# Loading v for two batches per transfer in an attention and spectral-mixing kernel

## The chip, the core and the metric

One core of a Trainium2 chip runs the whole kernel. TensorE (PE in the profile, with its weight loads as PEld), VectorE (DVE), ScalarE (ACT), GpSimd (POOL) and SyncE (SP) each run their own list of instructions in order; POOL and SP also issue the transfers between HBM and the on-chip memory, and 16 DMA engines carry them out. The metric is the device time of one execution in microseconds (us), taken as the median of the runs shown.

## What is computed

The reference, cut to what matters:

```python
scores = scale * q @ k.T                       # q, k, v: (8 batches, 8 heads, 576, 64), float32
cum = cumsum(log(clip(f, 1e-4, 1)))            # f: (8, 8, 576)
scores = where(causal, -1e9, scores + cum[..., :, None] - cum[..., None, :])
x = softmax(scores) @ v                        # then heads side by side: (8, 576, 512)
X = rfft(x, axis=1)[:, :64]                    # 64 modes
Y = X * (w_r + 1j * w_i)                       # per mode a 512 x 512 product, complex
u = x + irfft(Y)
out = u + relu(u @ w_ch)                       # (8, 576, 512), float32
```

The inputs are 9.4 MB each of q, k and v, and 134.2 MB of the mode weights w_r and w_i (64 modes x 512 x 512 x 4 bytes, twice).

## The kernel before

**Stages.** The kernel has two stages. The attention stage is the loop of L552 with 34 iterations over 32 pairs; a pair is one batch b and two neighbouring heads 2g and 2g+1 (L100: g outer, b inner, so pairs 2j and 2j+1 are two neighbouring batches of one g). Iteration i computes the scores and exponentials of pair i, the products with v of pair i-1, and the Fourier sums (`dft`) of pair i-2. The second stage (from L623) takes the mode products with the weights in 16 groups u of 4 modes, each group in four pieces dc, and the last part (from L845) builds the output. Some pieces of the weights are used early, within the attention loop: `spec_early` (L534) takes one from iteration 10 on, two in iterations 10 to 13.

**Transfers.** Nothing schedules the work: instructions stand in the order of the text, engine by engine. Except f and the first v, POOL issues every load; SP issues f, the first v and all stores. In iteration i of the attention loop the loads stand at its head, in this order:

- `load_qk(i + 4)` (L103): q and k of a pair, two transfers, converted to bf16 on the way, into one of 5 buffers. A buffer is free when `trans` (L346) of the pair five before it has read it.
- `issue_half()` (L174): half of a weight piece (512 KB as written, converted from float32), into one of NW = 7 buffers or into a "guest" place that is not used yet (L132).
- `load_v(i + 3)` (L114): v of a pair, float32, 288 KB, into one of 4 buffers. It is free when `scale_v` (L369) of pair i-1 has read it. `scale_v(i + 1)` stands at the end of iteration i.
- a second `issue_half()`, except in iterations 3, 6, 9, 12 and 15.

Before the loop (L229 to L238) SP issues f and v of pairs 0, 1 and 2, while POOL issues q and k of pairs 0 to 3 with three weight halves between them.

**Semaphores.** The framework gives POOL's transfers eight semaphores in turn, so POOL's next transfer waits until the one eight before it has landed; SP's take turns on eight others. In the second stage POOL issues a whole weight piece (two transfers) after each piece used (L814), and waits for the matmuls of `spec_mms` (L180) to free a buffer.

**What reads v.** `scale_v` on DVE multiplies v by a factor per row and writes `vn` in bf16 (L372); `turn_v` (L376) and `back_v` (L388) put `vn` through two transposes on PE into `vs`, the operand of the products of `av` (L469).

```python
        vt = vpool.tile([128, 9, Dh], F32, tag="vt", name="vt")
            v[b, 2 * g : 2 * g + 2, :, :].rearrange("h (c r) d -> (h c) (r d)", r=9),
```

Partition p of the tile holds nine rows r of 64 values: 2304 bytes that lie side by side in HBM, and the 128 partitions follow one another without a gap.

Of the kernel before, what the change touches and what calls it, by code (L numbers as in the profile page):

```python
# [10 lines left out]
F32 = mybir.dt.float32  # L11
BF16 = mybir.dt.bfloat16
I32 = mybir.dt.int32
ALU = mybir.AluOpType
# [3 lines left out]
def _strided(ap: bass.AP, free_dims, offset_elems: int = 0) -> bass.AP:  # L18
    new_ap = [list(ap.ap[0])] + [list(x) for x in free_dims]
    return bass.AP(tensor=ap.tensor, offset=ap.offset + offset_elems, ap=new_ap)  # L20
# [3 lines left out]
def kernel(  # L24
# [12 lines left out]
    B, H, S, Dh = q.shape  # L37
# [8 lines left out]
    NPAIR = B * H // 2  # L46
# [34 lines left out]
    wn = const.tile([128, NPAIR, 9], F32, name="wn")  # L81
# [4 lines left out]
    actx = ExitStack()  # L86
    ssb = actx.enter_context(tc.tile_pool(name="ssb", bufs=1))
    qkpool = actx.enter_context(tc.tile_pool(name="qkpool", bufs=5))
    vpool = actx.enter_context(tc.tile_pool(name="vpool", bufs=4))
    vnpool = actx.enter_context(tc.tile_pool(name="vnpool", bufs=2))  # L90
    vTpool = actx.enter_context(tc.tile_pool(name="vTpool", bufs=1))
    vspool = actx.enter_context(tc.tile_pool(name="vspool", bufs=2))
# [8 lines left out]
    st = [dict() for _ in pairs]  # L101

    def load_qk(i):  # L103
        g, b = pairs[i]
        qk = qkpool.tile([128, 2, S], BF16, tag="qk", name="qk")
        st[i]["qk"] = qk

        for n, src in enumerate((q, k)):
            nc.gpsimd.dma_start(  # L109
                qk[64 * n : 64 * n + 64, :, :],  # L110
                src[b, 2 * g : 2 * g + 2, :, :].rearrange("h (p r) d -> p h (r d)", p=64),
            )

    def load_v(i, eng=None):  # L114

        g, b = pairs[i]
        vt = vpool.tile([128, 9, Dh], F32, tag="vt", name="vt")
        st[i]["vt"] = vt
        (eng or nc.gpsimd).dma_start(
            vt[:].rearrange("p r d -> p (r d)"),  # L120
            v[b, 2 * g : 2 * g + 2, :, :].rearrange("h (c r) d -> (h c) (r d)", r=9),
        )


# [49 lines left out]
    def issue_half():  # L174
        issue_w(whalf[0])
        whalf[0] ^= 1
# [50 lines left out]
    nc.gpsimd.iota(s_i[:], pattern=[[128, NSB]], base=0, channel_multiplier=1)  # L227
    nc.gpsimd.iota(m_i[:], pattern=[[1, 128]], base=0, channel_multiplier=0)
    nc.sync.dma_start(ft, f.rearrange("b h s -> (b h) s"))  # L229
    for i in range(3):  # L230
        load_v(i, nc.sync)
    load_qk(0)
    issue_half()
# [34 lines left out]
    def setup_cum():  # L268
        nc.vector.tensor_tensor_scan(cum[:, 0:S], ones1, lf, 0.0, ALU.mult, ALU.add)
        rref = ssb.tile([BH, 1], F32, name="rref")  # L270
        nc.vector.tensor_copy(rref[:], cum[:, 256:257])
        nc.vector.tensor_scalar(cum[:, 0:S], cum[:, 0:S], rref[:], None, ALU.subtract)
        nc.vector.tensor_copy(cum[:, S : 2 * S], cum[:, 0:S])
        nc.vector.tensor_copy(cum[:, 2 * S : 2 * S + 64], cum[:, 512:576])
# [29 lines left out]
    def setup_small():  # L304
        nc.vector.tensor_scalar(trimask[:], m_f[:], s_f[:, 0:1], None, ALU.is_ge)
        nc.vector.memset(tri4[:], 0.0)
        nc.vector.tensor_copy(tri4[0:64, 0, :], trimask[0:64, 0:64])
        nc.vector.tensor_copy(tri4[64:128, 1, :], trimask[64:128, 64:128])

    def setup_basis():  # L310
        nc.vector.tensor_scalar(bas3[:, :, 0, :], Zt[:, :, :, 1], -1.0, None, ALU.mult)
        nc.vector.tensor_copy(bas3[:, :, 1, :], Zt[:, :, :, 0])
        nc.vector.tensor_copy(bas3[:, :, 2, :], Zt[:, :, :, 1])
# [51 lines left out]
    def widx(i):  # L365
        g, b = pairs[i]
        return 4 * b + g

    def scale_v(i):  # L369
        vn = vnpool.tile([128, 9, Dh], BF16, tag="vn", name="vn")  # L370
        st[i]["vn"] = vn
        nc.vector.tensor_tensor(  # L372
            vn[:], st[i]["vt"][:], _strided(wn[:, widx(i), :], [[1, 9], [0, Dh]]), ALU.mult
        )

    def turn_v(i):  # L376

        tv = psM.tile([128, 9, 64], BF16, tag="m", name="tv")
        for r in range(9):
            for hp in range(2):  # L380
                sl = slice(64 * hp, 64 * hp + 64)
                nc.tensor.transpose(tv[sl, r, :], st[i]["vn"][sl, r, :], ident_bf[sl, sl])  # L382
        st[i]["vT"] = vTpool.tile([128, S], BF16, tag="vT", name="vT")
        nc.vector.tensor_copy(  # L384
            st[i]["vT"][:].rearrange("p (c r) -> p c r", r=9), tv[:].rearrange("p r c -> p c r")
        )
# [25 lines left out]
    def scores(i, T):  # L412

        QT, KT = st[i]["T"][:, 0, :], st[i]["T"][:, 1, :]
        if T == 0:
            st[i]["et"] = epool.tile([128, 3, 2, 512], BF16, tag="et", name="et")
            st[i]["e4"] = epool.tile([128, 64], BF16, tag="e4", name="e4")
            st[i]["m4"] = epool.tile([128, 2, 64], BF16, tag="m4", name="m4")
        if T == 3:
            ps = psM.tile([128, 64], F32, tag="m", name="s4")  # L420
            for hp in range(2):
                sl = slice(64 * hp, 64 * hp + 64)
                nc.tensor.matmul(  # L423
                    ps[sl, :], lhsT=KT[sl, 512:576], rhs=QT[sl, 512:576], start=True, stop=True
                )
            nc.scalar.activation(st[i]["e4"][:], ps[:], ACT.Exp, scale=scale)  # L426
            return
        ps = psS.tile([128, 2, 512], F32, tag="S", name="sps")
        for jb, i0, n, c in SPANS[T]:
            for hp in range(2):  # L430
                sl = slice(64 * hp, 64 * hp + 64)
                nc.tensor.matmul(  # L432
                    ps[:, hp, c : c + n],
                    lhsT=KT[sl, jb * 128 : jb * 128 + 128],
                    rhs=QT[sl, i0 : i0 + n],
                    start=True,
                    stop=True,
                )
        nc.scalar.activation(st[i]["et"][:, T, :, :], ps[:], ACT.Exp, scale=scale)  # L439
# [29 lines left out]
    def av(i, sb):  # L469
        if sb in (0, 3):  # L470
            st[i]["pav"] = psV.tile([128, 3, 2, Dh + 1], F32, tag="av", name="pav")
        pav, vs = st[i]["pav"], st[i]["vs"]
        Ms = SBLK[sb]
        for hp in range(2):
            for jb in range(sb + 1):
                rhs = vs[:, 8, :] if jb == 4 else vs[:, 2 * jb + hp, :]
                nc.tensor.matmul(  # L477
                    pav[:Ms, sb % 3, hp, :],
                    lhsT=eblk(i, hp, jb, sb),
                    rhs=rhs,  # L480
                    start=(jb == 0),
                    stop=(jb == sb),
                )
# [68 lines left out]
    for i in range(NPAIR + 2):  # L552
        live = i < NPAIR
        if i + 4 < NPAIR:
            load_qk(i + 4)
        issue_half()
        if i + 3 < NPAIR:
            load_v(i + 3)
        if i not in less:
            issue_half()  # L560
        prev = i - 1 if 1 <= i <= NPAIR else None
        if live:
            scores(i, 0)
        if i == 0:
            setup_cum()
            setup_small()
        if prev is not None:
            av(prev, 0)
            av(prev, 1)
        if live:  # L570
            scores(i, 1)
        if 0 < i < NPAIR:
            turn_v(i)
        if prev is not None:
            av(prev, 2)
            norm(prev, 0)
        if i + 1 < NPAIR:
            trans(i + 1, 0)
        if live:
            scores(i, 2)  # L580
            if i == 0:
                setup_wn(0, 5)
                setup_wn(5, 9)
                scale_v(0)
                setup_w()
                turn_v(0)
            mask(i, 0)
        if prev is not None:
            av(prev, 3)
        if i + 1 < NPAIR:  # L590
            trans(i + 1, 1)
        if live:
            scores(i, 3)
            back_v(i)
        if prev is not None:
            av(prev, 4)
            norm(prev, 1)
        if live:
            mask(i, 1)
        if i + 1 < NPAIR:  # L600
            scale_v(i + 1)
        if i == 1:
            setup_basis()
        if 10 <= i < 14:
            spec_early(*early[spec_done])
            spec_done += 1
        if i >= 2:
            dft(i - 2)
        if i == 2:
            setup_late()  # L610
        if 3 <= i < 3 + NSB:
            setup_bi(i - 3)
        if i == 3 + NSB:
            setup_bi4(0, 512)
        if i == 4 + NSB:
            setup_bi4(512, 64)
        if i >= 10:
            spec_early(*early[spec_done])
            spec_done += 1
# [3 lines left out]
    with ExitStack() as bctx:  # L623
# [296 lines left out]
        for i in range(len(steps)):  # L920
# [13 lines left out]
            p, sb = steps[i][0]  # L934
# [59 lines left out]
```

## Time and profile before

| | |
|---|---|
| median of 3 runs | 437.77 us (437.42 to 439.06) |
| the profiled execution | 440.27 us |
| its span, first to last instruction | 438.5 us |
| mean granted TensorE clock | 0.938 of full speed |
| busy: PE, DVE, ACT, POOL | 348.4, 268.0, 234.8, 146.1 us |
| moved by the DMA engines | 96.75 MB in 68,414 packets |
| read from HBM, written to HBM | 163.73 MB, 9.44 MB |
| v loads by POOL | 29 of 288 KB, median 10.6 us from issue to landing |
| v loads by SP | 3 of 288 KB, median 7.3 us |

How to read it: a busy time is the sum of an engine's instructions, over stages with different limits. The DMA bytes are counted as written, so a load that turns float32 into bf16 counts half of what it reads; the HBM figure counts what is read. The DMA share adds the times of all packets over 16 engines; two packets of one engine can overlap, so it can exceed 1. In the chain of waits each step goes back to what released it. The attention loop runs from about 10 us to 235 us, the second stage to about 400 us, the output to the end.

### The profile page before, as it was taken

The page shows a single profiled execution, that of the slowest core. Times are in us where ns is not written, and L with a number is a line of the kernel's source. Part 1 is how long each engine was busy: PE and PEld are TensorE (multiplying, and loading weights), DVE is VectorE, ACT ScalarE, POOL GpSimd, SP SyncE. Part 2 cuts the span into 40 slices and gives each one's busy share as a digit, 9 for nine tenths or more (in the row PEclk, how much of TensorE's full clock was granted, in tenths as well). Part 3 has the DMA queues.
Part 4 walks back from the last instruction along what each step waited for, and adds up shares of the span by engine and source line. Part 5 has one row for each costly group of instructions (what it writes and reads, how often), then busy time and mean ns, then how long its engine had stood idle before and what let it go on. Part 6 is the DMA issues. An engine that isn't in the chain of part 4 may idle for free.

```text
span 438.5 us, 10295 instructions
## 1 busy us (share of the span) xinstructions
PE 348.4 (79%) x4264; PEld 191.7 (44%) x4274; DVE 268.0 (61%) x650; ACT 234.8 (54%) x359; POOL 146.1 (33%) x216
## 2 busy tenths in 40 slices
PE   1589877798988988989896484699888598889993
PEld 0355555555555555555563242243333233335330
DVE  4677888867788778888885231222233166455784
ACT  4455776777877756566561022034132166355883
POOL 6454444444544444344214111111122212100283
PEclk9999999999999999999999588599699599699998
DMA  8999999999999999999999999999999999995598
GB/s 180 205 232 221 230 222 232 228 230 228 230 231 224 228 223 227 224 224 223 230 215 212 212 212 212 213 211 212 212 211 212 210 209 210 210 210 106 193 341 331
DMA packets 68414, 96.75 MB, mean 221 GB/s; under 512 B 3600, under 2 KB 45072, under 8 KB 68368
## 3 DMA queue, kind: packets, MB, share of 16 engines
q0 software_dynamic: 62800, 85.64, 105.5%
q1 hardware_dynamic: 5568, 10.47, 6.6%
q8 instruction: 33, 0.54, 0.5%
q14 instruction: 13, 0.11, 0.1%
HBM read 163.73 MB, written 9.44 MB: 395 GB/s over the span
## 4 chain that ended last, share of the span: by engine, by line
PE 40%; DMA 32%; DVE 19%; ACT 3%; issue 3%; POOL 1%; POOLq 0%; ACTq 0%; DVEq 0%
DMA w<-in_moe_w_i_dram 22%; DMA w<-in_moe_w_r_dram 8%; PE pav L477 6%; DVE vT L384 5%; DVE qkT L360 5%; PE A L194 5%; DVE x_all L492 4%; PE pd L521 4%; PE sps L432 4%; PE tv L382 3%; PE vp L393 3%; DMA qk<-in_k_dram 2%; PE U L657 2%; PE s L423 2%; ACT e L426 2%
## 5 line engine op out<-in xcount | busy, mean ns | idle before, releaser
L439 ACT ACTIVATE et<-sps 128x1024 bf16<-128x1024 f32 x96 | 96.0, 1049 | 15.8 <-PE sps L432 12.8
L477 PE MATMUL pav<-vs,et 128*128 128x65 bf16 (+1 forms) x896 | 52.7, 200 | 0.2 <-DVE vn L372 0.2
L360 DVE COPY qkT<-tp 128x640 bf16<-128x640 bf16 x64 | 48.8, 764 | 4.8 <-PE tp L355 4.7
L818 DVE TENSOR_TENSOR Yb<-A,yx 128x512 bf16<-128x512 f32 x15 | 10.4, 691 | 61.6 <-PE A L194 61.6
L477 PEld LDWEIGHTS <-et 128*128 128x128 bf16 (+1 forms) x896 | 37.6, 104 | 18.2 <-issue 13.7
L432 PE MATMUL sps<-qkT 64*128 64x512 bf16 (+4 forms) x320 | 40.3, 315 | 1.1 <-DVE qkT L360 1.1
L697 PE MATMUL pxw<-wch,xT 128*128 128x512 bf16 (+1 forms) x152 | 39.5, 405 | 1.0 <-DVE xT L687 0.4
L194 PE MATMUL A<-w,XP 128*16 128x512 bf16 (+1 forms) x240 | 22.2, 453 | 21.8 <-DMA w<-in_moe_w_i_dram 14.1
L355 PE MATMUL tp<-ident_bf,qk 128*64 128x128 bf16 x576 | 30.6, 238 | 10.9 <-DMA qk<-in_k_dram 10.9
L492 DVE TENSOR_TENSOR x_all<-pav,rcp 128x384 bf16<-128x384 f32 (+2 forms) x96 | 36.2, 377 | 3.3
L384 DVE COPY vT<-tv 128x576 bf16<-128x576 bf16 x32 | 24.2, 757 | 19.7 <-PE tv L382 19.7
L165 POOL DMA_DIRECT2D w<-in_moe_w_r_dram x16 | 11.9, 742 | 70.6 <-PE A L194 50.8
L156 POOL DMA_DIRECT2D w<-in_moe_w_r_dram x27 | 20.4, 757 | 39.9 <-PE A L194 9.1
L704 ACT CAST XW<-pxw 128x512 bf16<-128x512 f32 (+1 forms) x16 | 9.3, 584 | 45.6 <-PE pxw L697 26.6
L404 ACT COPY vs<-vp 128x576 bf16<-128x576 bf16 x32 | 20.5, 639 | 21.9 <-PE vp L400 21.9
L704 ACT CAST yx<-pxw 128x512 bf16<-128x512 f32 (+1 forms) x24 | 14.0, 584 | 32.8 <-PE pxw L697 32.8
L109 POOL DMA_DIRECT2D qk<-in_q_dram x32 | 19.5, 611 | 35.1 <-DMA w<-in_moe_w_r_dram 8.4
L165 POOL DMA_DIRECT2D w<-in_moe_w_i_dram x19 | 13.3, 697 | 52.4 <-PE A L194 23.8
L744 ACT CAST x_all<-pu 128x512 bf16<-128x512 f32 (+1 forms) x40 | 23.4, 584 | 10.6 <-PE pu L743 9.8
L491 DVE RECIPROCAL rcp<-pav 128x6 f32<-128x6 f32 (+2 forms) x96 | 16.2, 169 | 17.7 <-PE pav L477 17.6
L156 POOL DMA_DIRECT2D w<-in_moe_w_i_dram x27 | 20.3, 752 | 18.5 <-DMA w<-in_moe_w_i_dram 8.0
L355 PEld LDWEIGHTS <-qk 128*64 128x64 bf16 x576 | 19.7, 117 | 14.8 <-issue 9.6
(149 smaller groups left out, 685.3 us busy)
## 6 DMA issues: line engine op xcount, KB each, us to landing
w<-in_moe_w_r_dram POOLq DMA_DIRECT2D x16, 1024.0 KB, 29.8
w<-in_moe_w_i_dram POOLq DMA_DIRECT2D x15, 1024.0 KB, 32.4
w<-in_moe_w_r_dram POOLq DMA_DIRECT2D x27, 512.0 KB, 10.9
w<-in_moe_w_i_dram POOLq DMA_DIRECT2D x27, 512.0 KB, 12.4
vt<-in_v_dram POOLq DMA_DIRECT2D x29, 288.0 KB, 10.6
out_dram<-o_sb SPq DMA_DIRECT2D x20, 256.0 KB, 3.2
qk<-in_q_dram POOLq DMA_DIRECT2D x32, 144.0 KB, 10.8
qk<-in_k_dram POOLq DMA_DIRECT2D x32, 144.0 KB, 10.6
```

The costliest lines, as they stand in the source:

```text
L156: nc.gpsimd.dma_start(w8[:, t, :, :], src[4 * u : 4 * u + 4, dc * 128 : (dc + 1) * 128, :].rearrange("m p e -> p m e"),)
L165: nc.gpsimd.dma_start(w8[:, j : j + step, :, :].rearrange("p m r e -> p m (r e)"), src[m : m + step, 256:512, :].rearrange("m (p r) e -> p ...
L194: nc.tensor.matmul(A[32 * j : 32 * j + M, :], lhsT=lhsT, rhs=rhs, start=st_, stop=sp_)
L355: nc.tensor.transpose(tp[64 * hp : 64 * hp + 64, r - r0, :, :].rearrange("p n c -> p (n c)"), qk[:, hp, r * 64 : r * 64 + 64], ident_bf[:, :],
L360: nc.vector.tensor_copy(st[i]["T"][:].rearrange("p n (c r) -> p n c r", r=9)[:, :, :, r0:r1], tp[:, 0 : r1 - r0, :, :].rearrange("p r n c ...
L384: nc.vector.tensor_copy(st[i]["vT"][:].rearrange("p (c r) -> p c r", r=9), tv[:].rearrange("p r c -> p c r"))
L432: nc.tensor.matmul(ps[:, hp, c : c + n], lhsT=KT[sl, jb * 128 : jb * 128 + 128], rhs=QT[sl, i0 : i0 + n], start=True, stop=True,)
L439: nc.scalar.activation(st[i]["et"][:, T, :, :], ps[:], ACT.Exp, scale=scale)
L477: nc.tensor.matmul(pav[:Ms, sb % 3, hp, :], lhsT=eblk(i, hp, jb, sb), rhs=rhs, start=(jb == 0), stop=(jb == sb),)
L492: nc.vector.tensor_tensor(x_all[:ns, g, b, lo:hi, :].rearrange("p s (h d) -> p s h d", h=2), pav[:ns, lo % 3 : lo % 3 + n, :, 0:Dh], _stri ...
L697: nc.tensor.matmul(pxw[rows, :], lhsT=xT[:, eb, sb * 128 : sb * 128 + Ms], rhs=wch[:, eb, :], start=(eb == 0), stop=(eb == NEB - 1),)
L744: nc.scalar.copy(x_all[rows, :, to, sb, :], pu[rows, :].rearrange("p (g c) -> p g c", g=NEB))
```

## The change

`load_v(i)` now loads v of pairs i and i+1 (two batches, the same two heads) in one transfer into a tile with twice the bytes per partition, of which there are two in place of four. SP issues two such loads in the setup, for pairs 0 to 3. In the loop the call stands at the same place, between the two weight halves, in odd iterations 1 to 27 only, for pairs i+3 and i+4. The memory taken is the same (4 x 2304 or 2 x 4608 bytes per partition). Each pair's `scale_v` reads its half of the tile.

```diff
-    vpool = actx.enter_context(tc.tile_pool(name="vpool", bufs=4))
+    vpool = actx.enter_context(tc.tile_pool(name="vpool", bufs=2))
...
         g, b = pairs[i]
-        vt = vpool.tile([128, 9, Dh], F32, tag="vt", name="vt")
-        st[i]["vt"] = vt
+        vt = vpool.tile([128, 2, 9, Dh], F32, tag="vt", name="vt")
+        for k in range(2):
+            st[i + k]["vt"] = vt[:, k, :, :]
         (eng or nc.gpsimd).dma_start(
-            vt[:].rearrange("p r d -> p (r d)"),
-            v[b, 2 * g : 2 * g + 2, :, :].rearrange("h (c r) d -> (h c) (r d)", r=9),
+            vt[:].rearrange("p b r d -> p b (r d)"),
+            v[b : b + 2, 2 * g : 2 * g + 2, :, :].rearrange("b h (c r) d -> (h c) b (r d)", r=9),
         )
...
-    for i in range(3):
+    for i in (0, 2):
         load_v(i, nc.sync)
...
-            vn[:], st[i]["vt"][:], _strided(wn[:, widx(i), :], [[1, 9], [0, Dh]]), ALU.mult
+            vn[:], st[i]["vt"], _strided(wn[:, widx(i), :], [[1, 9], [0, Dh]]), ALU.mult
...
         issue_half()
-        if i + 3 < NPAIR:
+        if i % 2 and i + 4 < NPAIR:
             load_v(i + 3)
         if i not in less:
             issue_half()
```

## The prediction

> **What bounds the kernel now.** I read the chain of waits first, then the DMA rows of the page, then the busy times by stage, then who waits on PE.
>
> The chain that ended last, on the page:
>
> ```profile
> PE 40%; DMA 32%; DVE 19%; ACT 3%; issue 3%; POOL 1%; POOLq 0%; ACTq 0%; DVEq 0%
> ```
>
> Its pieces from 230 us on, the longest of them (start, length, what):
>
> ```profile
> 239.96 34.21 DMA w<-in_moe_w_i_dram
> ...
> 275.58 33.20 DMA w<-in_moe_w_r_dram
> ...
> 310.11 33.56 DMA w<-in_moe_w_i_dram
> ...
> 344.20 29.46 DMA w<-in_moe_w_i_dram
> ...
> 373.70 0.96 PE A L194 x7
> ```
>
> From 240 to 373.7 us the chain is weight transfers alone: each is issued when a buffer comes free and lands some 30 us later. No v transfer stands in the chain. A compute tail follows. Is this a queue that waits for buffers or DMA engines that are full? The busy times by stretch answer (last two columns: DMA share and GB/s as written):
>
> ```profile
> 0.00:5.00 5.00, 0.00 (x0) 0.00 (x0) 3.75 (x10) 1.34 (x2) 4.13 (x12) 1.00 0.55 124
> 5.00:20.00 15.00, 5.90 (x70) 4.25 (x70) 7.33 (x18) 9.03 (x16) 7.24 (x11) 1.00 1.20 213
> 20.00:220.00 200.00, 171.92 (x2909) 112.24 (x2906) 160.81 (x435) 138.80 (x191) 88.61 (x136) 1.00 1.21 227
> 240.00:340.00 100.00, 74.49 (x512) 33.87 (x520) 25.81 (x52) 23.35 (x40) 16.21 (x22) 0.83 1.12 212
> 340.00:390.00 50.00, 40.55 (x229) 16.49 (x229) 23.77 (x38) 24.46 (x43) 8.11 (x13) 0.83 1.17 210
> ```
>
> The engines are full from 5 to 390 us. Counted as read, by the trace's packet records, they read 405 to 410 GB/s in every 20 us of the attention stage and 423 in the weight stage. So the last weight lands when all bytes have been moved, and the end moves only by what the change does to the engine time of the bytes, or by leaving engines empty. PE waits for weights:
>
> ```profile
> PE A L194 <- DMA w<-in_moe_w_i_dram: 14.1, 4, 4.3
> PE tp L355 <- DMA qk<-in_k_dram: 10.9, 2, 9.6
> PE A L194 <- DMA w<-in_moe_w_r_dram: 7.6, 5, 2.7
> ```
>
> The first and third row give 21.7 us: a small shift of the attention stage is taken up there, since weights, not PE, are late behind it.
>
> **The change part by part.**
>
> *POOL's issues.* Removed: 29 v issues of 0.559 us (16.2 us of POOL). Added: 14 of two pairs. Between 0.559 us (128 rows) and 0.757 us (the weight halves' issue, 512 rows) I take 0.62 for 256 rows, 8.7 us. POOL saves 7.5 us, worth nothing: in 20 to 220 us it is busy 88.6 of 200 us and otherwise waits for landings and buffers. SP issues two transfers where it issued three (1.51 us together), hidden too.
>
> *Bytes.* The same. The 28 pairs that POOL still loads are 1792 packets of 4608 bytes now (64 per pair in the records: two rows side by side in HBM). After it, rows of the two batches alternate, so no two neighbours are side by side. The q and k loads, whose rows of 2304 bytes alternate between heads, have one packet per row. I expect the same: 3584 packets of 2304 bytes. Price of a packet cut in two, from the records of stages that are full: 2060 packets of 2048 bytes in a 20 us stretch of the weight stage are 20,000 x 16 / 2060 = 155.3 ns each; a stretch with 1179 of 1024 and 1456 of 2048 bytes then gives (320,000 - 1456 x 155.3) / 1179 = 79.6 ns, so two halves cost 159.2, or 3.9 ns more. 1792 x 3.9 / 16 = **+0.4 us**. Bounds: in the same way the attention stretches give about 90 ns for a q or k row (2304 bytes read) and 203 for a v packet; two rows at 90 save 23 ns: 1792 x 23 / 16 = -2.6 us. Above, SP's rows of 2304 bytes took 123 ns on average against 184 for POOL's packet: +62 ns, over the overlap of 1.21: 1792 x 62 / 16 / 1.21 = +5.7 us. The cut weight packet is nearest, the same bytes in the same full queue.
>
> *Number of transfers.* 32 become 16. Each ends in 16 packets of 4 bytes (3088 and 512 in the records, 20 ns on average), one per engine: 16 x 20 ns = -0.3 us at most; over the overlap, and with 0 as the other end, I take **-0.2 us**.
>
> *Setup.* SP's queue carries 1152 KB in place of 864 while PE waits for the first k (the 10.9 us above, ending at 9.6 and 14.3 us). 288 KB at 285 GB/s, the slowest full microsecond there with SP rows alone, is 1.0 us; the other end is 0, if the queues take turns so that k lands first. The attention stage may start up to 1.0 us later. The 21.7 us hide it; without them it would cost 1.0 us. The bytes come off a later POOL load.
>
> *The new wait.* A v load waited for `scale_v` of pair i-1; now, in odd i, for pair i, one iteration later. Behind it on POOL stand a weight half and the next q and k. Before's issue times against the end of that `scale_v`; the tightest place:
>
> ```profile
> 131.29 0.56 POOL L119 DMA_DIRECT2D vt<-in_v_dram  x1 [0.20 <-DVE vn L372]
> ```
>
> ```profile
> 130.54 0.74 DVE L372 TENSOR_TENSOR vn<-vt,wn 128x576 bf16<-128x576 f32 x1
> ```
>
> The gate would open at 131.28 and POOL came at 131.29 (i = 17). Over i = 1, 3, ..., 27 the slack is 0.4, 0.35, 0.6, 2.1, 2.9, 1.4, 0.9, 0.7, 0.0, 2.0, 2.8, 3.3, 4.9, 6.1 us. But POOL will come earlier: its window of eight transfers now holds a weight half where it held a v, 1.05 MB read at 410 GB/s, 2.6 us. So it is held up to 2.6 us. While it is held the engines work off what is issued: 2.2 MB as read stood open at 130 us, 5.4 us of work, the same amount when the gate opens later in a deeper window. A transfer issued then needs some time before its bytes flow: f, alone, landed after 3.0 us, of which 0.36 is moving, so 2.6 us. 5.4 - 2.6 leaves a cushion of 2.8 us, at least the hold. **0**. The landing is in time: `scale_v` of pair i+3 comes 19 us behind the gate (6.35 us an iteration), a landing takes 10.6 to 12.5.
>
> Sum: +0.4 - 0.2 = +0.2 us on the profiled 440.27. Its median of three runs is 437.77, 2.5 us less, mostly the run's own spread (the clock granted to busy matmuls from 376 to 380 us was 0.50). On the median: **438.0 us**.
>
> **The rivals.**
>
> *Rows that run slower (slower).* If HBM serves two alternating places worse, each pair of rows may cost up to the 62 ns above: 437.8 + 5.7 = 443.5. It passes 0.5% (2.2 us) from 2.2 x 16 / 1792 = 20 ns per two rows. For it: SP's rows. Against: those were timed in the first 9 us, when a single packet per engine was open; half packets of weights pay 3.9 ns.
>
> *POOL held until the queue is dry (slower).* If the cushion is 1.4 us and not 2.8, the hold of 2.6 less the slack exceeds it at i = 1, 3, 5, 13, 15 and 17: 0.8 + 0.85 + 0.6 + 0.3 + 0.5 + 1.2 = 4.2 us, 442.0. It decides once the share of the DMA falls below 1.1 beside the new wait. Against: the smallest amount open at any time from 14 us on is 1.9 MB, 4.7 us.
>
> *Setup not hidden (slower, within the band).* 437.8 + 1.0 + 0.2 = 439.0.
>
> *Cheaper rows (faster).* If a v row costs what a q row does, -2.6 - 0.2: 435.0. Against: q and k write half the bytes.
>
> *A gap at each transfer (faster).* If the engines stood still between transfers, 16 fewer would each save the 2.6 us of f: 42 us, 396. The rows deny it: share 1.21, never under 1.9 MB open from 14 us on. The Trainium skill, "DMA: Bandwidth & Descriptors", section "Bandwidth", asks for transfers of at least 1 MiB, and its section "Anatomy of one DMA — SWDGE (gpsimd) path" gives about 2.0 us of fixed cost per transfer; by that, an estimate, 16 x 2.0 = 32 us less. In this trace the fixed part lies under the other seven transfers.
>
> **How the numbers follow.** Forecast 0.70; rows slower 0.10; queue dry 0.05; setup 0.03; cheaper rows 0.10; gaps 0.02. A measurement of this kernel can tell about 0.5%, 2.2 us, from no change. Faster: 0.10 + 0.02 = 0.12. Slower: 0.15. Same: 0.73. The range, 435.4 to 440.8, takes in nearly all of the cheaper rows below, and half of the slower rows and the dry queue above; what is left out is under 0.2. The forecast's own range is 436.8 to 439.2, the runs' spread.
>
> **What would show it.** The page's packets under 8 KB at about the same 68,400 + 1,800 - 250 (cut packets), or 1,800 fewer (not cut). The stretch 20 to 220 us still at a DMA share of 1.2 and about 227 GB/s; a lower figure there is the slower rows or the dry queue, told apart by POOL's waits on `vn`, which I expect under 2.6 us each, some 8 of them. The first k up to 1.0 us later. The chain from 240 to 374 us unchanged. Wrong if the wait of 373.7 moves by over 2 us, or the chain there no longer holds weight transfers.

## The result, and the profile after

| | before | changed |
|---|---|---|
| median of 22 runs each | 438.00 us | 439.47 us |
| the profiled execution, its span | 440.27, 438.5 us | 440.03, 437.8 us |

The ratio of the changed kernel to the one before is 1.0029 (95% interval 1.0019 to 1.0039): 1.3 us slower (0.8 to 1.7). A second measurement, e11 below, gave 1.0028 (1.0015 to 1.0042). The forecast was 438.0, +0.2 us, no change within 0.5%. The wide range (435.4 to 440.8) held, and so did "same". The forecast's own narrow range (436.8 to 439.2) did not, and a loss that is clear of noise was missed: the prediction took 0.5% for what can be told apart here, and the interval is 0.1% to either side.

One profile cannot show 1.3 us here: the two profiled executions stand the other way round, 437.8 against 438.5 us. The clock may be the reason. The changed kernel was profiled twice (the second time as e11 below). Both executions had read 163.6 of the 163.7 MB at 401.2 us, and yet the spans are 437.8 and 436.5 us. In the records the granted TensorE clock was halved for 6.8 us from 373.4 us on in the first and for 3.4 us from 373.9 us on in e11. The stretch around it, first profile and then e11; the third column from the end is the clock:

```profile
372.00:382.00 10.00, 8.21 (x35) 3.25 (x34) 3.79 (x7) 3.50 (x6) 1.61 (x3) 0.66 1.16 211
```

```profile
372.00:382.00 10.00, 8.47 (x50) 3.74 (x50) 4.55 (x8) 4.42 (x8) 1.61 (x3) 0.83 1.15 211
```

In the profiles of all runs, from there (163.6 MB read) to the end of the span it is 36.2 to 37.1 us in the five with the longer halved stretch, 34.8 to 36.3 in the seven with the shorter, and 35.3 and 36.4 in two with none. What the profile is good for is where things happen. The page of the changed kernel, packets and chain:

```profile
DMA packets 68221, 96.74 MB, mean 221 GB/s; under 512 B 3344, under 2 KB 44816, under 8 KB 68176
...
PE 36%; DMA 36%; DVE 17%; issue 4%; ACT 3%; POOL 1%; POOLq 0%; ACTq 0%; DVEq 0%
```

193 packets fewer, which is the prediction's case "not cut": the packet records have 1792 of 4608 bytes for POOL's v, 64 per pair as before. The two batches' rows lie apart in HBM, yet two rows are still one packet; the records do not say which two. Closing packets of 4 bytes went from 3600 to 3344, and SP's fourth pair adds 64, since SP sends rows singly.

The longest pieces of the chain from 230 us on:

```profile
240.07 33.65 DMA w<-in_moe_w_i_dram
...
274.72 33.59 DMA w<-in_moe_w_r_dram
...
309.72 33.26 DMA w<-in_moe_w_i_dram
...
343.51 29.45 DMA w<-in_moe_w_i_dram
...
373.00 0.80 PE A L195 x7
```

The same weight transfers end the same waits, at 373.0 (before: 373.7; the kernel before profiled again, e0: 372.4). The busy times by stretch (last two columns: DMA share, GB/s as written):

```profile
0.00:5.00 5.00, 0.00 (x0) 0.00 (x0) 3.75 (x10) 1.35 (x2) 4.13 (x12) 1.00 0.56 161
5.00:20.00 15.00, 6.59 (x80) 4.82 (x80) 8.18 (x20) 9.03 (x16) 7.34 (x12) 1.00 1.21 220
20.00:220.00 200.00, 172.50 (x2919) 112.50 (x2919) 160.40 (x437) 139.71 (x192) 83.30 (x122) 0.99 1.21 226
240.00:340.00 100.00, 75.97 (x508) 34.44 (x519) 25.45 (x52) 23.36 (x40) 16.30 (x22) 0.81 1.12 212
```

Full engines from 5 us on, 226 for 227 GB/s in the attention stage: averages that hide what follows. The first k came no later than one profile differs from the next: PE's first wait for it ends at 8.7 and 9.2 us in the two profiles of the changed kernel, at 9.6 and 8.6 in two of the kernel before (the second is e0). POOL's waits ahead of v loads that are put down to `vn`:

```profile
POOL vt L120 <- DVE vn L373: 3.6, 3, 1.5
```

Three waits, 3.6 us in all, at most 1.5: the new wait exists and is short. Start times say the same: four of the 14 issues (i = 1, 3, 7, 13) start 0.29 us behind the end of the `scale_v` that they wait for, the least distance in any profile of two pairs per load, and so were held; the other ten start later. In e11 it is one (i = 1).

### The profile page after: what moved, and what is told of

It reads as the page before. It is cut to its first block, busy times and chain, and to the rows that moved or that the text cites. A ratio compares the mean times of both kernels' runs of the same rounds, so it can differ in the third digit from the quotient of the medians.

```text
span 437.8 us, 10264 instructions
## 1 busy us (share of the span) xinstructions
PE 350.6 (80%) x4264; PEld 192.7 (44%) x4274; DVE 267.5 (61%) x650; ACT 234.7 (54%) x359; POOL 140.2 (32%) x201
## 2 busy tenths in 40 slices
DMA packets 68221, 96.74 MB, mean 221 GB/s; under 512 B 3344, under 2 KB 44816, under 8 KB 68176
## 4 chain that ended last, share of the span: by engine, by line
PE 36%; DMA 36%; DVE 17%; issue 4%; ACT 3%; POOL 1%; POOLq 0%; ACTq 0%; DVEq 0%
DMA w<-in_moe_w_i_dram 22%; DMA w<-in_moe_w_r_dram 12%; PE pav L478 5%; DVE qkT L361 4%; DVE x_all L493 4%; DVE vT L385 4%; PE A L195 4%; PE sps L433 4%; PE tv L383 3%; PE pd L522 3%; PE vp L394 3%; DMA qk<-in_k_dram 2%; PE U L658 2%; PE Z L658 2%; ACT e L427 1%
## 5 line engine op out<-in xcount | busy, mean ns | idle before, releaser
L478 PEld LDWEIGHTS <-et 128*128 128x128 bf16 (+1 forms) x896 | 37.6, 104 | 18.3 <-issue 13.7
L698 PE MATMUL pxw<-wch,xT 128*128 128x512 bf16 (+1 forms) x152 | 41.1, 418 | 1.0 <-DVE xT L688 0.4
L493 DVE TENSOR_TENSOR x_all<-pav,rcp 128x384 bf16<-128x384 f32 (+2 forms) x96 | 36.2, 377 | 3.3
L157 POOL DMA_DIRECT2D w<-in_moe_w_r_dram x27 | 20.5, 759 | 41.6 <-DMA w<-in_moe_w_i_dram 10.0
L405 ACT COPY vs<-vp 128x576 bf16<-128x576 bf16 x32 | 20.5, 639 | 22.0 <-PE vp L401 22.0
L109 POOL DMA_DIRECT2D qk<-in_k_dram x32 | 19.1, 598 | 27.6 <-DMA w<-in_moe_w_r_dram 17.4
L688 DVE COPY xT<-ptr 128x576 bf16<-128x576 bf16 x32 | 14.6, 457 | 18.8 <-PE ptr L683 18.1
```

The costliest lines, as they stand in the source:

```text
L157: nc.gpsimd.dma_start(w8[:, t, :, :], src[4 * u : 4 * u + 4, dc * 128 : (dc + 1) * 128, :].rearrange("m p e -> p m e"),)
L478: nc.tensor.matmul(pav[:Ms, sb % 3, hp, :], lhsT=eblk(i, hp, jb, sb), rhs=rhs, start=(jb == 0), stop=(jb == sb),)
L493: nc.vector.tensor_tensor(x_all[:ns, g, b, lo:hi, :].rearrange("p s (h d) -> p s h d", h=2), pav[:ns, lo % 3 : lo % 3 + n, :, 0:Dh], _stri ...
L698: nc.tensor.matmul(pxw[rows, :], lhsT=xT[:, eb, sb * 128 : sb * 128 + Ms], rhs=wch[:, eb, :], start=(eb == 0), stop=(eb == NEB - 1),)
```

## The experiments

All ratios are to the kernel before, timed beside it on the same chip, with 95% intervals. "Outside the span" is the device time less the span from the first to the last instruction.

### e0: the kernel before against itself

No edit.

> The kernel before, unchanged, timed against itself. Every theory expects a ratio of 1.000 within about 0.1%; it shows how far two timings of one kernel lie apart, and what its execution takes outside the span from the first to the last instruction (1.8 us in the one profile of before, 2.2 us in all 22 executions of the changed kernel).

Measured: 0.9999 (0.9988 to 1.0009). Outside the span 1.82 us on average. So 0.3% can be told, and the 0.4 us outside the span (2.22 us on average in the changed kernel) are real.

### e1: only the setup part

```diff
-    for i in range(3):
+    for i in range(4):
         load_v(i, nc.sync)
...
-        if i + 3 < NPAIR:
+        if i and i + 3 < NPAIR:
             load_v(i + 3)
```

> Only the setup part: SP issues v of pairs 0 to 3 as four single transfers, iteration 0 loads none, from iteration 1 on all as before (four single buffers). Theory SETUP (the 1.3 us come from what SP's larger share does to the start): +1.3 us. Theory LOOP (they come from the loads of two pairs in odd iterations): 0. Theory CLOCK (a shift of the stages against the windows in which the clock is cut, whatever caused it): some value from 0 to 1.3 us, tied to how far the stages move.

Measured: 1.0024 (1.0013 to 1.0034). That looks like theory SETUP, but the profile puts part of it at the far end. SP's waits in e0, then in e1 (who waited for what: us in total, times, longest):

```profile
SPq L989 <- DMA out_dram<-o_sb: 2.1, 3, 0.9
```

```profile
SPq L989 <- DMA out_dram<-o_sb: 2.5, 1, 2.5
```

At the end SP looks at its eight semaphores in order. With 32 transfers the last store is on the eighth; with 33 it is on the first, and the other seven are looked at after it has landed, 0.43 us in all. From the last store's bytes to the end of the span it is 1.69 us in e1, 1.27 in e0 and, with 31 transfers and the last store on the seventh, 1.34 in the changed kernel. So 0.4 of e1's 1.1 us belong to its own count of transfers and are not part of the changed kernel's loss. Another 0.2 us lie outside the span (2.03 us on average). In the attention stage e1 loses nothing (table below), and the rest of its loss has no place.

### e2: only the loop part

SP loads v of pairs 0, 1 and 2 singly, POOL that of pair 3 in iteration 0; then as changed. `load_one(i, vt)` loads one pair into its half of a double buffer.

```diff
-    for i in (0, 2):
-        load_v(i, nc.sync)
+    vt0 = [vpool.tile([128, 2, 9, Dh], F32, tag="vt", name="vt") for _ in range(2)]
+    for i in range(3):
+        load_one(i, vt0[i // 2], nc.sync)
...
+        if i == 0:
+            load_one(3, vt0[1])
         if i % 2 and i + 4 < NPAIR:
```

> Only the loop part: SP issues v of pairs 0, 1, 2 singly and POOL that of pair 3 in iteration 0, as before; from iteration 1 on one transfer for two pairs in odd iterations into two double buffers. Theory SETUP: 0. Theory LOOP: +1.3 us. Theory CLOCK: between.

Measured: 1.0045 (1.0029 to 1.0061), 2.0 us. The loop part costs. The two parts together (1.0024 and 1.0045) cost more than the whole change (1.0029), so its loss cannot be shared out between them by these ratios.

### e3: the two pairs in two transfers

```diff
-        (eng or nc.gpsimd).dma_start(
-            vt[:].rearrange("p b r d -> p b (r d)"),
-            v[b : b + 2, 2 * g : 2 * g + 2, :, :].rearrange("b h (c r) d -> (h c) b (r d)", r=9),
-        )
+        for k in range(2):
+            load_one(i + k, vt, eng)
```

> The changed kernel with each transfer of two pairs given back as two single transfers at the same place (SP four singles, POOL two in each odd iteration), the same two double buffers and the same wait. If the larger transfer itself costs (its order of rows, its one completion for two pairs): 0 against before. If the place and the earlier wait for the buffer cost: +1.3 us. SETUP: +1.3 us.

Measured: 1.0057 (1.0037 to 1.0076). So it is not the larger transfer; two ordinary ones at the same place cost as much or more (SP's 33 transfers, as in e1, are in it). The place or the wait remained.

The packet records then told where. Reads in GB/s in stretches of the attention stage, all 405 to 410 on average:

```
                48:51  88:90  126:129 us
e0 (before)      394    400    412
changed          375    376    383
e2               378    378    401
e3               385    392    354
e4 (below)       402    386    410
```

In the changed kernel single microseconds fall to 346, 361 and 351 GB/s, at 49, 50 and 88 us. A single low microsecond proves little: the first profile of the kernel before has 356 and 361 at 192 and 193 us. POOL's issues ahead of the first dip:

```profile
38.34 0.71 POOL L120 DMA_DIRECT2D vt<-in_v_dram  x1 [0.91 <-DVE rep L322]
39.05 0.61 POOL L109 DMA_DIRECT2D qk<-in_q_dram  x1
40.02 0.60 POOL L109 DMA_DIRECT2D qk<-in_k_dram  x1 [0.37 <-DMA w<-in_moe_w_i_dram]
42.56 0.76 POOL L157 DMA_DIRECT2D w<-in_moe_w_r_dram  x1 [1.94 <-DMA yx<-in_moe_w_r_dram]
```

v of two pairs is followed directly by q and k. That happens only where a v load falls into an iteration that issues one weight half: 3, 9 and 15. Their loads land at 49, 88 and 127 us. The change had put the v loads into odd iterations, and three of the five short iterations are odd. This became theory NEIGHBOUR, against GATE (the earlier wait) and END (the 0.4 us outside the span).

### e4: three transfers by SP in the setup

```diff
-    for i in (0, 2):
-        load_v(i, nc.sync)
+    load_v(0, nc.sync)
+    vt2 = vpool.tile([128, 2, 9, Dh], F32, tag="vt", name="vt")
+    for i in (2, 3):
+        load_one(i, vt2, nc.sync)
```

> The changed kernel with SP's part of the setup as three transfers in place of two: pairs 0 and 1 in one, pair 2 and pair 3 singly into the halves of the second double buffer. SP then issues 32 transfers in all, as before, and not 31. Theory END (0.4 us of the 1.26 lie outside the span, 2.2 us in place of 1.8, and go with SP's number of transfers, which decides on which of its eight semaphores the last store stands): outside the span 1.8 us again, and 0.4 us less than the changed kernel: +0.8 us against before. Theory LOOP alone: outside 2.2 us, +1.3 us.

Measured: 1.0013 (0.9997 to 1.0030), outside the span 1.87 us. It fits END, but e7 contradicts it. Nor does e4 speak clearly for NEIGHBOUR, which was not among its theories: iterations 3, 9 and 15 are as in the changed kernel, yet of the three dips its profile has only the second (386 GB/s in the table), and its interval reaches from no loss to that of the changed kernel.

### e5: a weight half behind every v

```diff
-    less = (3, 6, 9, 12, 15)
+    less = (2, 6, 8, 12, 14)
```

> The changed kernel with the iterations that issue one weight half moved from 3, 6, 9, 12, 15 to 2, 6, 8, 12, 14, so that a weight half always follows the load of two pairs. Theory NEIGHBOUR (in iterations 3, 9 and 15 the two pairs' v is followed by q and k with no weight half between; there, and in no other place, the reads fall to 346 to 382 GB/s for one to three microseconds, at 49, 88 and 127 us, some 0.6 us in all): these dips go, 0.5 us less than the changed kernel: +0.8 us against before. Theory GATE (POOL's wait for scale_v costs): no change, +1.3 us.

Measured: 0.9991 (0.9976 to 1.0006). The loss is gone: its interval and that of the changed kernel (1.0019 to 1.0039) do not meet. The stretch at the second dip, changed kernel and then e5:

```profile
88.00:90.00 2.00, 1.93 (x25) 0.92 (x21) 1.66 (x6) 1.74 (x3) 0.77 (x1) 1.00 1.15 221
```

```profile
88.00:90.00 2.00, 1.79 (x42) 1.31 (x37) 1.83 (x4) 2.00 (x3) 0.26 (x2) 1.00 1.21 199
```

Read the next-to-last column: 1.15 against 1.21. The GB/s are higher in the dip because v counts fully as written and converted bytes by half; as read it is 376 against 395. e5 keeps the wait, and its longest wait put down to `vn` is 2.0 us, longer than the changed kernel's 1.5.

The v packets show the place too. On average over a load of two pairs they took 209, 204 and 211 ns in the loads of iterations 3, 9 and 15 of the changed kernel and 180 to 190 in its other eleven; in e5 all 14 loads lie between 180 and 187.

### e6: v behind the second weight half

```diff
-        if i % 2 and i + 4 < NPAIR:
-            load_v(i + 3)
         if i not in less:
             issue_half()
+        if i % 2 and i + 4 < NPAIR:
+            load_v(i + 3)
```

> The changed kernel with the load of two pairs behind the second weight half of its odd iteration, so that q and k of the next iteration follow it directly in all 14 cases. Theory NEIGHBOUR: 14 dips of some 0.2 us in place of three, about 2 us more than the changed kernel: +3 us against before. Theory GATE: POOL reaches the wait one weight half later (some 2.5 us) and is not held any more, and one instruction less stands behind it: equal to or faster than the changed kernel, +0.5 to +1.3 us.

Measured: 1.0052 (1.0033 to 1.0072), 2.3 us. POOL's waits on `vn` ahead of v loads shrink to one:

```profile
POOL vt L120 <- DVE vn L373: 0.2, 1, 0.2
```

The wait is all but gone and the kernel is slower still: GATE falls, and e7 below goes against it as well. All 14 loads now have q and k behind them. The loss is less than 14/3 of that of three cases, and below the 3 us that NEIGHBOUR expected, so the dips are not all alike (microseconds below 372 GB/s at 35, 50, 64, 65, 164 and 171 us, not at every load).

### e7: e4 and e5 together

> The changed kernel with both: three transfers by SP in the setup, and one weight half in iterations 2, 6, 8, 12 and 14. If END and NEIGHBOUR both hold, 0.9 us less than the changed kernel: +0.3 us against before. If neither does, +1.3 us.

Measured: 0.9987 (0.9971 to 1.0003). Outside the span 2.27 us, with SP's 32 transfers: END falls. The neighbour part alone gives what e5 gave. POOL's waits on `vn` ahead of v loads are the longest of all here:

```profile
POOL vt L120 <- DVE vn L384: 10.0, 5, 3.4
```

The kernel that waits most at the new gate has the lowest ratio.

### e8: the even iterations in the kernel before

The edit of e5, made to the kernel before.

> Control: the kernel before (one pair per transfer, every iteration) with the single weight half in iterations 2, 6, 8, 12, 14 in place of 3, 6, 9, 12, 15. In both, five v loads of one pair are followed directly by q and k. Theory NEIGHBOUR: no change, ratio 1.000. If the moved weight halves are themselves worth something, whatever v does: faster by the 0.4% that they were worth in the changed kernel.

Measured: 1.0007 (0.9989 to 1.0024). Moving the short iterations is worth nothing by itself; it helps only where it parts v of two pairs from q and k.

### e9: five odd short iterations

```diff
-    less = (3, 6, 9, 12, 15)
+    less = (3, 5, 9, 11, 15)
```

> The changed kernel with the single weight half in iterations 3, 5, 9, 11, 15 (all odd): five loads of two pairs, and not three, are followed directly by q and k. Theory NEIGHBOUR: two more dips of 0.15 to 0.2 us each, 0.3 to 0.4 us more than the changed kernel, and seven odd-even steps above the kernel with even ones: +0.4% against before. Theory GATE and all that do not count neighbours: equal to the changed kernel, +0.3%.

Measured: 1.0047 (1.0033 to 1.0060) beside 1.0028 for e11, measured next to it. The new dips stand where iterations 5 and 11 put them; e9:

```profile
61.00:63.00 2.00, 2.00 (x26) 1.25 (x28) 1.49 (x7) 1.57 (x3) 0.77 (x1) 1.00 1.15 233
...
100.00:102.00 2.00, 1.93 (x32) 1.13 (x33) 1.38 (x8) 1.30 (x3) 0.00 (x0) 1.00 1.14 223
```

The same stretches of the changed kernel:

```profile
61.00:63.00 2.00, 2.00 (x24) 1.19 (x22) 1.37 (x7) 1.13 (x2) 0.76 (x1) 0.94 1.18 260
...
100.00:102.00 2.00, 1.63 (x26) 1.02 (x25) 1.41 (x7) 0.88 (x3) 0.06 (x1) 1.00 1.16 248
```

As read these are 367 and 377 GB/s in e9, 409 and 405 in the changed kernel. Of the three old places two show again (372 and 381 in the stretches of the table); the first reads 399.

### e10: v ahead of the only weight half

```diff
-        issue_half()
+        if not (i % 2 and i in less):
+            issue_half()
         if i % 2 and i + 4 < NPAIR:
             load_v(i + 3)
+        if i % 2 and i in less:
+            issue_half()
```

> The changed kernel with v of two pairs ahead of the only weight half in iterations 3, 9 and 15 (q, k, v, v, weight; before it q, k, weight, v, v and then q, k). v then follows q and k directly, and a weight half follows v. If any direct neighbourhood of v with q and k costs: equal to the changed kernel, +0.3%. If only q and k behind v cost (nothing but short rows and POOL's waits until the next weight half): the gain of the even iterations, 0.3 to 0.4% less, -0.1 to 0%.

Measured: 1.0005 (0.9995 to 1.0015). In time, v between k and a weight half is nearly harmless, and q and k directly behind v cost. The reads are not as clear: with v ahead there are dips too, now where the early loads land (371 GB/s from 45 to 47 us, 400 in the changed kernel; 398 and 386 from 84 to 87 and 122 to 125 us, 409 and 408 there), and the v packets of these three loads took 208, 196 and 202 ns. So the dips alone do not make up the loss.

### e11: the changed kernel again

> The changed kernel itself once more, on the chip and beside the runs of before that the other three share: +0.29% by the first measurement (0.19 to 0.39). Theory NEIGHBOUR expects its three dips again behind iterations 3, 9 and 15, at about 49, 88 and 127 us.

Measured: 1.0028 (1.0015 to 1.0042). The dips at 49 and 88 us stand again (380 and 368 GB/s in the stretches of the table), that at 127 us does not (412).

The time from 10 to 92 MB read, by the packet records, one profile each, beside the ratio:

```
e7 200.61 0.9987 | e5 200.63 0.9991 | e1 200.68 1.0024 | e8 200.92 1.0007
before 200.98 (e0), 201.35 (first profile) | e4 201.11 1.0013 | e10 201.15 1.0005
e2 201.31 1.0045 | changed 201.43, 201.35 (e11) 1.0029 | e9 201.69 1.0047
e3 201.77 1.0057 | e6 202.62 1.0052
```

But for e1, whose cost lies elsewhere, and for small swaps, the order of the times is that of the reading. One kernel's two profiles differ by up to 0.4 us, so a single difference here proves little. Counted from the start of the span, 92 MB were read at 229.2 and 229.0 us in the changed kernel, at 229.8, 228.9 and 229.2 in the three profiles with one pair per transfer (the first, e0, e8), and at 228.4 and 228.3 in e5 and e7. So the profiles show that e5 and e7 read earlier than the changed kernel. They do not show that the changed kernel reads later than the kernel before.

## Why the prediction was right in kind, and where it was wrong

**What bounds the kernel: right.** The DMA engines stay full from 5 to 390 us, the chain ends in the same weight transfers, and what most runs gained or lost follows the time that the attention stage's bytes take.

**POOL's issues: right in effect.** A load of two pairs takes POOL 0.714 us, not 0.62; POOL's busy time fell by 5.9 us (146.1 to 140.2) and bought nothing.

**Bytes, the +0.4 us: wrong.** The packets were not cut. 1792 of 4608 bytes stayed, so this term is 0. The analogy with q and k did not hold. The rivals of slower and of cheaper rows, which priced cut rows, fall with it. (For the slower rows, "a single packet per engine" in the first 9 us was misread as well: the DMA share was 1.10 from 5 to 7 us and 1.16 from 7 to 9.) That the sum of +0.2 us came within 1.3 us of the result is no merit of its terms: one is 0, the other was not seen, and the wide range was drawn for rivals that fell.

**Number of transfers, -0.2 us: not told apart.** The closing packets went as counted, 256 fewer. The rival that every transfer leaves a gap is refuted: 16 fewer transfers did not save 42 us, nor the estimate of 32 us that I made from the Trainium skill's fixed cost per transfer ("DMA: Bandwidth & Descriptors", section "Anatomy of one DMA — SWDGE (gpsimd) path").

**Setup, up to 1.0 us later: did not appear** at the start of the attention stage, as the first k at 8.7 and 9.2 us shows.

**The new wait at 0: right.** It held POOL three or four times, by the rows for at most 1.5 us (I expected some eight below 2.6); e6, nearly without it, was slower, and e7, with most of it, was not. The rival of a queue that runs dry because POOL is held has no support: by issues and packet records 2.2 MB as read or more stood open in the changed kernel from 14 us on (1.8 before), and 2.8 or more in its three dips.

**The step that failed** is in what the sum leaves out. It has a price by kind of packet and none for what stands next to what, and gives no reason for that. The prediction even says what follows the load, "Behind it on POOL stand a weight half and the next q and k", and this is not so in iterations 3, 9 and 15, which issue only one weight half. The load was checked against what it waits for and not against what follows it. In three of 14 places the change took the weight half between v and the next q and k away from twice the v. e5 took that back and won 0.38% (1.0029 to 0.9991), and e7 and e10 won as much or nearly so; e9 made it five places and read 0.19% above e11 (the intervals, 1.0033 to 1.0060 and 1.0015 to 1.0042, overlap, the two new dips are where they should be); e8 shows that the moved weight halves alone are worth nothing.

**What stays open.** That the order of the loads decides is shown by the times of e5, e7, e8 and e10. How it does is not. In the dips the v packets take longer while the DMA share falls; the records do not name the engine, so whether single engines ran out of work cannot be seen. By the three stretches of the table the dips cost 3 x 32/407 + 2 x 31/407 + 3 x 24/407 = 0.6 us; by the time from 10 to 92 MB, against the mean of three profiles of one pair per transfer (e0, the first one and e8) it is 0.3 us, of the 1.3. Another 0.4 us lie outside the span (2.22 us on average, 1.82 before); they differ from kernel to kernel (1.82 to 2.27 us), and the number of SP's transfers, which I tried, does not set them. The rest I cannot place. Theory CLOCK is open for it: the mean granted clock is the same in the executions of both kernels (0.940 in 22 of the changed one, 0.941 in 29 of the one before, beside e0), but a halved stretch that lasts 3.4 us more or less at 373 us went with 1.3 us of span in two profiles of the changed kernel, as much as the whole loss, and how often each length comes was not counted. A third double buffer, which would take the wait away altogether, wasn't tried: the memory of the core has no room for it.

No version is shown to beat the kernel before: e7 and e5 have intervals that reach across 1.

## What to carry to other kernels

Where the DMA engines are the bound, merging transfers removes instructions and not time. When a load moves in a hand-written order, list what stands directly before and behind it in its queue in every iteration, the irregular ones first: here putting a weight half back behind v in three of 14 places took away the whole loss. Then test the order alone, in the changed kernel and in the one before.

## What the runs showed of the hardware

- A transfer of [128 partitions, 2 batches, 576] float32, rows of one partition apart in HBM and together in the tile, went in packets of 4608 bytes from POOL and of 2304 from SP (576 in the records, 64 of them f's). Rows that lie together in HBM had given the same sizes.
- v packets of two pairs took longer where q and k stood directly behind them or, in e10, directly ahead: on average over all loads 181 ns in e5 and e7, 186 in e10, 187.5 in the changed kernel, 190 in e9, 193 in e6. With one pair per transfer it was 184 and 185. Over the whole run the means for packets of weights, q and k stayed within 1 ns.
- In e9 just the loads of iterations 3, 5, 9, 11 and 15 stand out: 192, 203, 206, 205 and 218 ns, against 180 to 186 in the other nine.
- The end of this kernel depends in part on which of eight semaphores the last store stands on: 1.27 us from its last byte to the end of the span on the eighth (e0; 1.26 in e7), 1.69 on the first (e1). It is not all: e2 and e4, also on the eighth, took 1.55, with 0.3 us more in the very last step.
- In these records the granted clock falls to half for 3.4, 6.8, 10.2, 13.7, 17.1 or 20.5 us, but for stretches that the end of the span cuts off. Two executions of one kernel can differ in it: 6.8 and 3.4 us at 373 us in two profiles of the changed kernel, with spans of 437.8 and 436.5 us.
